# Seven quarter products in the second token-mixing product, and VectorE instructions merged over two PSUM banks or two sets

## The chip, the cores and the metric

One core of one Trainium2 chip. Times are device microseconds (us) of one execution; each quoted time is the median of the runs named beside it. PE is TensorE, DVE VectorE, ACT ScalarE, POOL GpSimd. PSUM is the memory that the kernel's matmuls write; the kernel uses it as eight banks of 512 f32 a partition. SBUF is where the kernel keeps everything else that it has on the chip.

## The reference

Eight batches of 1024 positions by 512 features. Each batch is an attention with projected keys and values, then a mixer with a token half and a channel half:

```python
k_proj = einsum('ks,bhsd->bhkd', E, k); v_proj = einsum('ks,bhsd->bhkd', F, v)
x  = softmax(q @ k_proj.T / sqrt(64)) @ v_proj          # heads side by side: (8, 1024, 512)
h  = maximum(x.T @ w_tok1, 0) @ w_tok2                  # w_tok1 1024 x 256, w_tok2 256 x 1024
u  = x + h.T
return u + maximum(u @ w_ch1, 0) @ w_ch2                # w_ch1 512 x 1536, w_ch2 1536 x 512
```

The product that this change is about is the second one of the token half, `... @ w_tok2`.

## The kernel before

A program of three layers matters here. First, every piece of work is a *job* with an engine, a price in us and a priority; a planner written in Python simulates the engines with these prices and fixes, before anything is built, one order of instructions for each engine.

```python
MM = {512: 0.216, 256: 0.109, 130: 0.057, 128: 0.057, 64: 0.057}
def pe(n, cols, fn, **kw):
    t = n * MM[cols]
    return pl.add("PE", t, t, fn, **kw)
def dve(cols, fn, ps=True, **kw):
    t = cols / 960 + 0.07 if ps else cols / 1920 + 0.07
    return pl.add("DVE", t, t + 0.09, fn, **kw)
```

Second, the two channel products and, from batch 2 on, the first token product are already done in seven quarter products where a plain blocked product has eight. This costs sums and differences of quarters: those of a weight are made once and kept in SBUF, those of the activations are made for each batch on VectorE (those for the first channel product are called S below). Several products of a set are added up in one bank; ScalarE first copies one bank into another to start it, which is called the seed copy. The sums of the first token weight, made once in batch 1:

```python
def tok1_sums():
    a11, a12, a21, a22 = [tok1_quarter(t, half) for t in range(2) for half in range(2)]
    ...
    one(5, wS[:, 0], a21, a22, add=True, after=kp_all)
    one(7, wS[:, 2], a11, a21)
    one(6, wS[:, 1], wS[:, 0], a11, deps=(5,))
    one(3, a21, a12, wS[:, 1], deps=(6, 7, 5), after=["wt1"])   # the fourth goes over a quarter of the weight
```

Third, the second token product, which is still the plain one. Output row `si` of a position takes every eighth column of the weight, so the weights have a step of 8 elements:

```python
def token2(b, si, due):
    def mm():
        for t in range(TC):                                    # TC = 2
            nc.tensor.matmul(bank(bk), wt2_sb[:, t, si::NSI], hT_sb[:, t, :], ...)   # 512 columns, NSI = 8
    pe(TC, 512, mm, ...)
    dve(512, lambda: nc.vector.tensor_add(out=u_t[b % 2][:, si, :], in0=bank(bk), in1=x_sb[:, si, :]), ...)
    # [cut] after four rows: transposition of u by DMA
```

Two other places are touched. The attention of a head is normalised in two halves (a reciprocal of 4 and a product of 256 for each), and the four sums of hidden quarters, `G`, that a set of the channel product ends with are made for one set at a time:

```python
    total(3, g21, G[:, 2, cs], True, [q21, g(2)])      # g21 has a buffer of its own
    total(5, G[:, 0, cs], g21, False, [q21, g(0)])
    total(4, G[:, 3, cs], G[:, 0, cs], False, [g(3), g(0)])
    total(6, G[:, 1, cs], G[:, 4, cs], False, [g(1), g(4)])
```

The softmax here doesn't subtract the row's maximum and nothing guards it: scores larger than these inputs give would overflow.

Of the kernel before, what the change touches and what calls it, by code (L numbers as in the profile page):

```python
# [12 lines left out]
ACT = mybir.ActivationFunctionType  # L13
EARLY = 12.0
SUMS = 60.0
FMAX = 3.4028234663852886e38

# [11 lines left out]
class Bank:  # L29


    def __init__(self, stream, full=True, seeded=False):
        self.stream, self.full, self.seeded = stream, full, seeded
        self.jobs, self.at = [], None
        self.read, self.write = [], []


class Planner:
# [37 lines left out]
    def plan(self):  # L76
# [36 lines left out]
        def home(b, now):  # L113

            if held[b.stream] == self.caps[b.stream]:
                return None
            if b.stream in "UD" and turn[b.stream][0] is not b:
                return None
            best = None
            keep = [i for i in self.homes["U"] if clean[i] and bank_free[i] is not None]  # L120
            if all(clean[:5]):
                keep = []
            for i in self.homes[b.stream]:
                t = bank_free[i]
                if t is None or (b.seeded and not clean[i]):
                    continue
                if not b.seeded and clean[i] and keep and keep[-1] == keep[0] == i:
                    continue
                c = (max(now, t), clean[i], t, i)
                if best is None or c < best:  # L130
                    best = c
            return best

        while any(can.values()):
# [26 lines left out]
            if j.takes:  # L161
                b = j.takes[0]
                b.at = spot
                turn[b.stream].remove(b)
                held[b.stream] += 1
                bank_free[spot] = None
            for b in j.banks:
                left[id(b)] -= 1
                if not left[id(b)]:
                    held[b.stream] -= 1  # L170
                    bank_free[b.at] = max(x.end for x in b.jobs) + 0.1
                    clean[b.at] = b.full
            order.append(j)
# [10 lines left out]
def kernel(  # L184
# [13 lines left out]
    nc = tc.nc  # L198
# [40 lines left out]
    def tile_of(shape, dtype, name):  # L239
        return sb.tile(shape, dtype, tag=name, name=name)  # L240

    banks = [ps.tile([P, S2], F32, tag=f"ps{i}", name=f"ps{i}") for i in range(8)]

    def bank(b):

        return banks[b.at]

# [33 lines left out]
    G_t = [tile_of([P, 7, C2, 2 * P], BF16, f"G{i}") for i in range(2)]  # L281
    a_t = [tile_of([P, S2], BF16, f"a{i}") for i in range(4)]
    rdn_t = [tile_of([P, 4], F32, f"rdn{i}") for i in range(4)]
    ub_t = [tile_of([P, 2, 2 * P], F32, f"ub{i}") for i in range(2)]
    ua_t = [tile_of([P, 2, 2 * P], F32, f"ua{i}") for i in range(2)]
    g21_t = [tile_of([P, 2, 2 * P], BF16, f"g21{i}") for i in range(2)]
    da = tile_of([P, 2, DH], F32, "da")
    ident32 = da[:KP, 0, :KP]
    db = tile_of([P, 2, DH], F32, "db")

# [285 lines left out]
    def scores(h, due):  # L576
        bk = Bank(stream[0], full=False)
        pe(
            1, 512,
            lambda: nc.tensor.matmul(  # L580
                bank(bk), kT[:, h].rearrange("p c k -> p (c k)"),
                qT[:, h].rearrange("p j s -> p (j s)"), start=True, stop=True,
            ),
            reads=[("kT", 0, h), ("kT", 1, h), ("qT", h)], takes=[bk], prio=due,
            after=[("a", h % 4)],
        )
        act(
            512,
            lambda: nc.scalar.activation(out=a_t[h % 4], in_=bank(bk), func=ACT.Exp, scale=scale),  # L589
            writes=[("a", h % 4)], uses=[bk],  # L590
        )

    def attend(h, half, due):
        bk = Bank(stream[0], full=False)
        rdn = rdn_t[2 * (h % 2) + half]

# [3 lines left out]
        def mm():  # L600
            for jj in range(2):
                j = 2 * half + jj
                nc.tensor.matmul(  # L603
                    view()[:, 2 * jj : 2 * jj + 2].rearrange("p c d -> p (c d)"),
                    a_t[h % 4][:, j * P : (j + 1) * P],
                    vb[:, h].rearrange("k c d -> k (c d)"), start=True, stop=True,
                )
# [19 lines left out]
        )  # L627

    def token1(t, due):
        bk = Bank(stream[0], full=False)  # L630
# [17 lines left out]

    def token2(b, si, due):
        bk = Bank(stream[0], full=False)  # L650

# [18 lines left out]
        if si % NJ == NJ - 1:  # L670
            i = si // NJ
            j = sp(
                3.5,
                lambda: nc.sync.dma_start_transpose(
                    out=uT_t[i].rearrange("p s dc q -> p (s dc) q"),
                    in_=u_t[b % 2][:, i * NJ : (i + 1) * NJ].rearrange("p s d -> p (s d)"),
                ),
                reads=[("u", b % 2, n) for n in range(i * NJ, (i + 1) * NJ)],
                writes=[("uT", i, n) for n in range(HP)], prio=None,
            )  # L680

            if b > 1:
                j.lat += 3.0
            turned_u[b, i] = j

# [49 lines left out]
    def token1_seven(b, due):  # L735
# [35 lines left out]
        def product(n):  # L771
            bb = bk["y" if X_OF[n] == "y" else "x"]
            src = rows[n] if n in T else xs[{1: 11, 2: 21, 3: 22}[n]]
            w = [("wS", n)] if n in (5, 6, 7, 3) else ["wt1"]
            pe(
# [40 lines left out]
        product(4)  # L816
        both(1, 0, ub, rows[6][0])

    def token1_pair(hp, due):
# [103 lines left out]
    def up_set(j, m):  # L923
# [3 lines left out]
        bk = {n: Bank("U", seeded=n == "y") for n in "xyz"}  # L927
        ub, ua, g21 = ub_t[s % 2], ua_t[s % 2], g21_t[s % 2]

# [41 lines left out]

        def total(n, in0, in1, add, deps):
            f = nc.vector.tensor_add if add else nc.vector.tensor_sub
            dve(
                512, lambda: f(out=G[:, n, cs], in0=in0, in1=in1), ps=False, reads=deps,  # L975
                writes=[g(n)],
            )
# [18 lines left out]
        relu(1, "y")  # L996
        product(4)
        dve(
            512, lambda: add_relu(g21, view("z"), ub), reads=[("ub", s % 2)],
            writes=[("g21", s % 2)], uses=[bk["z"]],  # L1000
        )
        q21 = ("g21", s % 2)
        total(3, g21, G[:, 2, cs], True, [q21, g(2)])
        total(5, G[:, 0, cs], g21, False, [q21, g(0)])
        total(4, G[:, 3, cs], G[:, 0, cs], False, [g(3), g(0)])
        total(6, G[:, 1, cs], G[:, 4, cs], False, [g(1), g(4)])

    out_v = out.rearrange("b (p si) d -> b p si d", p=P)

    def down_block(j):  # L1010
# [63 lines left out]
        def add_u(dst, key, src, sh, dh):  # L1074
# [3 lines left out]
            )  # L1078

        product(1, 0)  # L1080
        act(
# [5 lines left out]
        if last:  # L1087
            return finish(p6, product, add_u, store, bk, view, o_of, o_key)
        add_u(db, "db", "y", 1, 0)
        product(2, 3)  # L1090
        add_u(o_of(0, 0), o_key(0, 0), "x", 0, 0)
        product(5, 4)
        dve(
            512, lambda: nc.vector.tensor_add(out=da, in0=view("y"), in1=u_of(1, 1)),
            reads=u_key(1), writes=["da"], uses=[bk["y"]],
        )
        dve(
            512, lambda: nc.vector.tensor_add(out=o_of(1, 1), in0=view("z"), in1=da),
            reads=["da"], writes=[o_key(1, 1)], uses=[bk["z"]],
        )  # L1100
        product(3, 5)
        add_u(o_of(0, 1), o_key(0, 1), "y", 0, 1)
        store(0)
        product(4, 6)
        dve(
            512, lambda: nc.vector.tensor_add(out=o_of(1, 0), in0=view("z"), in1=db),
            reads=["db"], writes=[o_key(1, 0)], uses=[bk["z"]],
        )
        store(1)

    def finish(p6, product, add_u, store, bk, view, o_of, o_key):
# [12 lines left out]
        follow(p5[0], p6[1])  # L1124
        add_u(da, "da", "y", 1, 1)
        da_w = add(da, "da", "w", da, "da")
        follow(product(2, 4)[0], p5[1])
        c22 = add(o_of(1, 1), o_key(1, 1), "z", da, "da")
        store(1, (1,))
        follow(add_u(dc, ("ub", 0), "y", 0, 1), da_w)  # L1130
        follow(add_u(db, "db", "y", 1, 0), c22)
        follow(add_u(o_of(0, 0), o_key(0, 0), "x", 0, 0), c22)
# [4 lines left out]
        product(4, 6)  # L1137
        add(o_of(1, 0), o_key(1, 0), "z", db, "db")
        store(1, (0,))
# [36 lines left out]
    def front(b, begin, end):  # L1176
# [20 lines left out]
        for h in range(H):  # L1197
            if h + 2 < H:
                unit(0.4, lambda t, h=h: scores(h + 2, t))
            for half in range(2):  # L1200
                unit(0.25, lambda t, h=h, half=half: attend(h, half, t))
# [3 lines left out]
        else:  # L1205
            unit(3.2, lambda t: token1_seven(b, t))
        for si in range(NSI):
            unit(0.55, lambda t, si=si: token2(b, si, t))
        total = sum(c for c, _ in units)
# [8 lines left out]
    for b in range(B):  # L1218
# [5 lines left out]
        if b == 1:  # L1224
            tok1_sums()
        if b + 1 < B:
            at = 2 * TU * (b + 1)
# [58 lines left out]
```

## Time and profile before

| | before |
|---|---|
| time | 423.75 us (423.72 to 423.80, 3 runs) |
| TensorE | 413.8 us busy, 98% of the span |
| VectorE | 341.3 us busy, 81%, 837 instructions |
| ScalarE | 227.1 us busy, 54% |
| waits of TensorE from 110 us on | none listed |

The lines are in the prediction below. Read them so: the row of tenths says where in the span an engine is full, the chain of waits says which engine the end depends on, and a table of stretches gives busy time of each engine in a part of the span. Records of TensorE overlap (four matmuls of 256 columns are recorded as 0.60 us, and the next begins 0.44 us after their start), so I go by starts: what a start comes later than 0.109 us (after a matmul of 256 columns) or 0.215 us (after one of 512) is a wait. I call this the excess of a matmul.

### The profile page before, as it was taken

What the parts mean: (1) busy time and instruction counts of PE and PEld (TensorE: products, weight loads), DVE (VectorE), ACT (ScalarE), POOL (GpSimd) and SP (SyncE); (2) the same over time, 40 slices, a digit from 0 to 9 for tenths busy, and PEclk for the clock granted to TensorE, in tenths of its full rate; (3) what the DMA queues carried; (4) which work ended last, traced back from release to release, by engine and by line L of the source; (5) the groups of instructions that cost most, each with busy time, mean ns of one, the idle gap of its engine ahead of it and who ended that gap; (6) DMA issues with size and microseconds to landing.
All of it is one profiled execution on the core that took longest, in us unless ns stands there. A gap on an engine that the chain in (4) does not pass through costs nothing.

```text
span 421.8 us, 9380 instructions
## 1 busy us (share of the span) xinstructions
PE 413.8 (98%) x3778; PEld 343.0 (81%) x3778; DVE 341.3 (81%) x837; ACT 227.1 (54%) x434; POOL 66.3 (16%) x104
## 2 busy tenths in 40 slices
PE   8899999999999999999999999999999999999996
PEld 4587887788788878888788877889788888888885
DVE  2469979689799978799779887899778897878684
ACT  2858885357656454655446455564636544354430
POOL 8453220021111211020121200220100100010010
PEclk9999999999999999999999999999999999999999
DMA  9999999979999889959987699979930502250223
GB/s 168 207 201 206 207 207 165 240 121 209 173 155 219 138 192 176 151 152 149 202 139 158 110 169 225 146 156 152 200 75 2 151 2 99 51 151 6 95 96 106
DMA packets 96651, 62.47 MB, mean 148 GB/s; under 512 B 62048, under 2 KB 92256, under 8 KB 96608
## 3 DMA queue, kind: packets, MB, share of 16 engines
q0 software_dynamic: 34944, 45.09, 54.2%
q1 hardware_dynamic: 61584, 16.52, 22.5%
q8 instruction: 29, 0.48, 0.5%
q10 hardware_dynamic: 80, 0.26, 0.2%
q14 instruction: 14, 0.11, 0.1%
HBM read 59.24 MB, written 16.78 MB: 180 GB/s over the span
## 4 chain that ended last, share of the span: by engine, by line
PE 88%; DVE 5%; DMA 4%; POOL 1%; issue 1%; ACT 0%; POOLq 0%; DVEq 0%
PE ps L1041 34%; PE ps L940 33%; PE ps L654 6%; PE ps L764 4%; PE ps L603 3%; PE ps L580 3%; DMA q_sb<-in_q_dram 3%; PE ps L467 3%; DMA v_sb<-in_v_dram 2%; DVE u L867 1%; PE ps L634 1%; DVE x_sb L620 1%; PE ps L564 1%; DVE u L746 1%; PE ps L470 0%
## 5 line engine op out<-in xcount | busy, mean ns | idle before, releaser
L1041 PEld LDWEIGHTS <-G 128*128 128x128 bf16 x1344 | 129.8, 98 | 18.8 <-issue 0.3
L1041 PE MATMUL ps<-wc_sb,G 128*128 128x256 bf16 x768 | 103.1, 273 | 0.1
L962 ACT ACTIVATE G<-ps 128x512 bf16<-128x512 f32 x96 | 57.0, 597 | 70.6 <-PE ps L940 70.3
L940 PEld LDWEIGHTS <-wc_sb 128*128 128x128 bf16 x768 | 74.3, 98 | 12.0 <-issue 0.2
L1041 PE MATMUL ps<-wT,G 128*128 128x256 bf16 x576 | 77.7, 273 | 0.0
L940 PEld LDWEIGHTS <-wT 128*128 128x128 bf16 x576 | 55.3, 98 | 10.3 <-issue 1.0
L940 PE MATMUL ps<-uT,wc_sb 128*128 128x256 bf16 x384 | 57.7, 273 | 0.0
L940 PE MATMUL ps<-S,wc_sb 128*128 128x256 bf16 x384 | 57.6, 273 | 0.0
L940 PE MATMUL ps<-S,wT 128*128 128x256 bf16 x384 | 54.7, 273 | 0.4 <-DVE S L697 0.4
L1070 POOL DMA_DIRECT2D out_dram<-o x30 | 16.3, 545 | 219.8 <-DVE o L1076 133.5
L620 DVE TENSOR_TENSOR x_sb<-ps,rdn 128x256 bf16<-128x256 f32 x128 | 49.9, 416 | 0.6
L968 ACT COPY ua<-ps 128x512 f32<-128x512 f32 x48 | 28.2, 587 | 32.6 <-PE ps L940 32.2
L589 ACT ACTIVATE a<-ps 128x512 bf16<-128x512 f32 x64 | 37.3, 599 | 14.6 <-PE ps L580 14.1
L665 DVE TENSOR_TENSOR u<-ps,x_sb 128x512 bf16<-128x512 f32 x56 | 36.3, 686 | 10.2 <-PE ps L654 9.8
L921 DVE CUSTOM_DVE_ANT_0 g<-ps,ub 128x512 bf16<-128x512 f32 x48 | 32.9, 687 | 11.8 <-PE ps L940 11.6
L921 DVE CUSTOM_DVE_ANT_0 G<-ps,ua 128x512 bf16<-128x512 f32 x48 | 32.8, 684 | 10.4 <-ACT ua L968 10.4
L975 DVE TENSOR_TENSOR G<-G 128x512 bf16<-128x512 bf16 x96 | 39.4, 420 | 1.8
L615 DVE RECIPROCAL rdn<-ps 128x4 f32<-128x4 f32 x128 | 20.7, 175 | 15.5 <-PE ps L603 13.3
L968 ACT COPY ub<-ps 128x512 f32<-128x512 f32 x48 | 28.1, 586 | 9.0 <-PE ps L940 8.6
L603 PE MATMUL ps<-vb,a 128*128 128x130 bf16 x256 | 31.2, 220 | 0.0
L981 ACT COPY ps<-ps 128x512 f32<-128x512 f32 x48 | 27.8, 580 | 5.5 <-PE ps L940 3.1
L654 PE MATMUL ps<-hT_sb,wt_sb 128*128 128x512 bf16 x112 | 29.9, 379 | 0.0
(90 smaller groups left out, 527.3 us busy)
## 6 DMA issues: line engine op xcount, KB each, us to landing
out_dram<-o POOLq DMA_DIRECT2D x30, 512.0 KB, 4.0
k_sb<-in_k_dram POOLq DMA_DIRECT2D x14, 512.0 KB, 7.7
v_sb<-in_v_dram POOLq DMA_DIRECT2D x14, 512.0 KB, 9.7
q_sb<-in_q_dram POOLq DMA_DIRECT2D x14, 512.0 KB, 9.7
wc_sb<-in_moe_w_ch_dram POOLq DMA_DIRECT2D x6, 256.0 KB, 12.3
wc_sb<-in_moe_w_ch_dram POOLq DMA_DIRECT2D x4, 384.0 KB, 12.2
k_sb<-in_k_dram POOLq DMA_DIRECT2D x4, 256.0 KB, 6.7
v_sb<-in_v_dram POOLq DMA_DIRECT2D x4, 256.0 KB, 7.2
```

The source lines that it names most:

```text
L589: lambda: nc.scalar.activation(out=a_t[h % 4], in_=bank(bk), func=ACT.Exp, scale=scale),
L603: nc.tensor.matmul(view()[:, 2 * jj : 2 * jj + 2].rearrange("p c d -> p (c d)"), a_t[h % 4][:, j * P : (j + 1) * P], vb[:, h].rearrange("k ...
L620: lambda: nc.vector.tensor_tensor(out=x_sb[:, 4 * half : 4 * half + 4, h * D : (h + 1) * D], in0=view()[:, :, 0:D], in1=rdn[:, :, None].to ...
L654: nc.tensor.matmul(bank(bk), wt2_sb[:, t, si::NSI], hT_sb[:, t, :], start=(t == 0), stop=(t == TC - 1),)
L665: lambda: nc.vector.tensor_add(out=u_t[b % 2][:, si, :], in0=bank(bk), in1=x_sb[:, si, :]),
L921: nc.vector._custom_dve(TENSOR_ADD_SAT, out=out, in0=in0, in1=in1, s0=FMAX, s1=0.0)
L940: nc.tensor.matmul(t[:, c, :], w1_of(n, dd, 2 * m + c), a_of(j, n, dd), start=(n in (1, 7) and c == 0 and dd == 0), stop=(c == 1 and dd == 1),
L962: lambda: nc.scalar.activation(out=G[:, n, cs], in_=view(src), func=ACT.Relu),
L968: 512, lambda: nc.scalar.copy(out=dst, in_=view("y")), writes=[(name, s % 2)],
L975: 512, lambda: f(out=G[:, n, cs], in0=in0, in1=in1), ps=False, reads=deps,
L981: 512, lambda: nc.scalar.copy(out=view("y"), in_=view("x")), takes=[bk["y"]],
L1041: nc.tensor.matmul(view(where[n])[:, t, :], G[:, G_OF[n], cc, t * P : (t + 1) * P], w2_of(n, cc), start=(n in opens and t == 0 and cc == 0 ...
```

## The change

Its intent: TensorE sets the time, so take columns away from it. The second token product of batches 3 to 7 goes to seven quarter products of half the columns, in two sets of rows. That gives VectorE more to do, and to make room its other instructions are merged: a head's attention is normalised over two PSUM banks in one go, two rows of the plain second product are added in one go (batch 2), and the sums of `G` are made for two sets at once. For the two-bank instructions all of PSUM becomes one tile; for room in SBUF four buffers go (`da`, `db` and two of `g21`), and `g21` is computed in place in `G[5]`.

```diff
-        q21 = ("g21", s % 2)
-        total(3, g21, G[:, 2, cs], True, [q21, g(2)])
...
+        both = TOTALS[m] if SINGLE <= j < NSB - 1 else (m,)
+        if both:
+            total(3, 5, 2, True)
+            total(5, 0, 5, False)
...
+    wt2_v = wt2_sb.rearrange("p t (a i sh r) -> p t i sh r a", i=2, sh=2, r=2)
+    def tok2_sums():
+        for i in range(2):
+            a11, a12, a21, a22 = [wt2_v[:, t, i, sh] for sh in range(2) for t in range(2)]
+            def one(n, out, in0, in1, add=False, deps=(), after=(), i=i):
+                dve(512, lambda: f(out=out, in0=in0, in1=in1), ps=False, prio=SUMS + 50, ...)
+            waits = [("wait", 0), ("wait", 1)]
+            one(5, wS2[:, 0, i], a21, a22, add=True, after=waits)
+            one(7, wS2[:, 2, i], a11, a21, after=waits)
+            one(6, wS2[:, 1, i], wS2[:, 0, i], a11, deps=(5,), after=waits)
+            one(3, a21, a12, wS2[:, 1, i], deps=(6, 7, 5), after=["wt2"])
...
+    def token2_set(b, i, due, ...):
+        product(1); act(512, copy of x's bank into y's bank)
+        product(7); product(6); from_x(kept[0], ..., "y", 1, 0)
+        product(2); ...; product(5); ...; product(3); ...; product(4); ...
...
+            if b >= WHOLE:                      # WHOLE = 3
+                unit(0.5, lambda t, h=h: attend_whole(h, t))
...
+        if b == 2:
+            tok2_sums()
```

(The lines of `token2_set` are shortened here.) Three of the four sums of a set go into `wS2`, which shares its bytes with the buffer `wait`; the fourth goes over a quarter of the weight itself. `wait` is in use by the output blocks of the first batches, so the sums can only come when these are through with it.

## The prediction

> **What bounds the kernel now**
>
> I read the page first (busy shares, slices, chain), then the table of stretches, then the list of waits, then two short pieces of the timeline for the real cost of one instruction. From the page:
>
> ```profile
> PE 413.8 (98%) x3778; PEld 343.0 (81%) x3778; DVE 341.3 (81%) x837; ACT 227.1 (54%) x434; POOL 66.3 (16%) x104
> PE   8899999999999999999999999999999999999996
> DVE  2469979689799978799779887899778897878684
> ...
> PE 88%; DVE 5%; DMA 4%; POOL 1%; issue 1%; ACT 0%; POOLq 0%; DVEq 0%
> PE ps L1041 34%; PE ps L940 33%; PE ps L654 6%; PE ps L764 4%; PE ps L603 3%; PE ps L580 3%; DMA q_sb<-in_q_dram 3%; PE ps L467 3%; DMA v_sb<-in_v_dram 2%; DVE u L867 1%; PE ps L634 1%; DVE x_sb L620 1%; PE ps L564 1%; DVE u L746 1%; PE ps L470 0%
> ```
>
> TensorE (PE) is busy from the second slice to the last but one, and 88% of the chain that ended last is its matmuls. VectorE (DVE), which most of the diff is about, has 5% of that chain. The DMA share of the chain is the first 24 us (loads of k, v, q), which the change leaves alone.
>
> Busy is not dense, since PE records overlap. So the table of stretches, one of 49 us for each batch, which is the period of the kernel:
>
> ```profile
> 110.00:159.00 49.00, 49.00 (x434) 40.06 (x432) 42.31 (x105) 26.96 (x51) 6.70 (x10) 1.00 0.95 177
> 257.00:306.00 49.00, 49.00 (x444) 41.50 (x443) 41.77 (x102) 26.74 (x50) 6.72 (x10) 1.00 0.91 171
> 306.00:355.00 49.00, 49.00 (x439) 42.15 (x437) 42.19 (x104) 25.00 (x47) 2.13 (x4) 1.00 0.24 69
> ```
>
> The columns are window, length, then PE, PEld, DVE, ACT, POOL busy, then clock, DMA share and GB/s. PE has no gap in 49 us, at full clock; DVE has about 42 of 49 (86%). DMA share falls from 0.91 to 0.24 in the last stretch and the PE does not go faster for it, so the loads don't pace it either. The list of waits, asked for PE alone from 110 us to the end, names no wait at all.
>
> The timeline of PE shows how dense it is:
>
> ```profile
> 304.13 0.60 PE L764 MATMUL ps<-u,wt_sb 128*128 128x256 bf16 x4
> 304.57 1.04 PE L940 MATMUL ps<-S,wT 128*128 128x256 bf16 x8
> 305.44 0.82 PE L1041 MATMUL ps<-wc_sb,G 128*128 128x256 bf16 x6
> 306.10 1.46 PE L654 MATMUL ps<-hT_sb,wt_sb 128*128 128x512 bf16 x6
> 307.39 0.27 PE L940 MATMUL ps<-S,wc_sb 128*128 128x256 bf16 x1
> ```
>
> Take starts, not durations: eight 256-column matmuls in 305.44 - 304.57 = 0.87 us, 0.109 us each; six of 512 columns in 307.39 - 306.10 = 1.29 us, 0.215 us each. That is what the PE pays for a column whatever the product. The same reading for DVE:
>
> ```profile
> 328.48 0.42 DVE L975 TENSOR_TENSOR G<-g,G 128x512 bf16<-128x512 bf16 x1
> 328.81 0.69 DVE L1106 TENSOR_TENSOR o<-ps,db 128x512 f32<-128x512 f32 x1
> 329.41 0.17 DVE L615 RECIPROCAL rdn<-ps 128x4 f32<-128x4 f32 x1
> 329.50 0.40 DVE L975 TENSOR_TENSOR G<-G 128x512 bf16<-128x512 bf16 x1
> 329.81 0.18 DVE L615 RECIPROCAL rdn<-ps 128x4 f32<-128x4 f32 x1
> 329.90 0.73 DVE L620 TENSOR_TENSOR x_sb<-ps,rdn 128x256 bf16<-128x256 f32 x2
> 330.54 0.42 DVE L975 TENSOR_TENSOR G<-G 128x512 bf16<-128x512 bf16 x1
> ```
>
> Start to start: 512 bf16 within SBUF 0.33 us, 512 from PSUM 0.60, a reciprocal of 4 about 0.09, 256 from PSUM 0.32. About 0.09 us of each recorded duration lies under the next instruction. So merging two DVE instructions saves less than the durations suggest.
>
> [...] Splitting one of 512 in two costs only some 2 ns, so a product with 7/8 of the columns costs nearly 7/8 of the time.
>
> [...] The second token product takes its weights with a step of 8 elements, and its weight loads last longer (the L654 PEld group has 144 ns, the others 98 ns). Under a 215 ns matmul that hides; under 109 ns it might not. The trace has the harder case: L855 uses the same strided weights with 128-column matmuls, and the chain of waits has it at 16 in 0.98 us, 0.061 us each. So at 109 ns it is hidden.
>
> ```profile
> 26.42 0.98 PE ps L855 x16
> ```
>
> [...]
>
> **The change part by part**
>
> PE. The second token product (L654) of batches 3 to 7 goes to seven quarter products in two sets. Before, per batch: 8 x 2 = 16 matmuls of 512, 16 x 0.215 = 3.44 us. After: 2 sets x 7 products x 2 = 28 of 256, 28 x 0.109 = 3.05 us. Saved 0.39 us, times five batches 1.95 us. Nothing else on the PE changes: the merged attention keeps its four matmuls a head, and the instruction lists have 3838 matmuls against 3778, exactly 5 x (28 - 16) more. The first token product was already in seven parts from batch 2 on. All of the 1.95 us lies on the path.
>
> DVE occupancy, start to start; [...]256 bf16 at 0.20, 1024 bf16 at 0.60 (as the first token product's differences have it):
> - Attention over two banks, 40 heads: before 2 x (0.09 + 0.32) = 0.82, after 0.09 + 0.60 = 0.69. Saves 0.13 x 40 = 5.2 us.
> - Sums of G over two sets, 13 blocks: before 12 x 0.33 = 3.96, after 4 x 0.60 + 4 x 0.33 = 3.72. Saves 0.24 x 13 = 3.1 us.
> [...]
> - Seven products, 5 batches: before 8 x 0.60 = 4.80; after 4 differences x 0.20 + 12 additions from PSUM x 0.60 = 8.00. Adds 3.2 x 5 = 16 us.
> - Sums of the second weight, once, 8 strided instructions of 256 elements[...]: 8 x 0.33 adds 2.6 us.
>
> Sum: +10 us of DVE over the run. Per batch from 3 on: -1.0 -0.5 +3.2 = +1.7 us, so from 42 of 49 to about 44 of 48.6, or 90%. The instruction count falls (837 to 749 in the lists), but the load rises: the merging pays for half of what the seven products cost. ACT gains one copy of 0.58 us a set, 5.8 us in all, at 54% load.
>
> Path: 423.75 - 1.95 = 421.8. I add 0.2 us for new short waits in ten sets: 422.0.
>
> **The rivals**
>
> 1. DVE becomes the bound. At 90% it isn't on average. But the second token product crowds the last fourth of a batch's preparation: 8.0 us of its own in about 12 us, beside a base (up, down and S sums, about half of DVE's time) of 6 us, so about 2 us too much there. If the PE had to wait for it in each of the five batches: 421.8 + 5 x 2 = 432, slower by 2%. Against: u is needed late. In the trace the first transposition of u is issued at 309.2 us, lands 4.2 us later, and the first S sum that reads it starts at 320.0, over 6 us of slack; and the next batch's projection, which follows, needs no DVE. Partly true would be 0.3 us a batch, 423.3.
>
> 2. The seeded chain. In each set one PSUM bank is filled, read, added to, read and added to again, so three products of a set each wait for a DVE or ACT read of 0.6 us plus signalling. Ten sets x 4 turnarounds x 0.3 us exposed would be 12 us, 434. Against: the order of the PE's instructions puts 4 to 18 other matmuls (0.4 to 2 us) between most dependent products, and the first token product has the same chain now and shows no wait.
>
> 3. The saving is hidden, because loads or something else sets the period: 423.75, no change. Against: no PE wait from 110 us on, and the transfers wait for buffers that PE frees.
>
> 4. The rearrangement also removes the small PE waits before 110 us (some 1.6 us between 40 and 113 us by starts). Then 420.5 or so. Only the plan of batch 2 changes there, so I give it little.
>
> **Range and chances**
>
> The saving is known to a tenth; what is open is the waits, more likely added than removed. Predicted 422.0 us, 421.0 to 423.6 in 8 of 10. Faster by over 2% would need 8.5 us, which the change takes nowhere: 0.5%. Slower by over 2% needs rival 1 or 2 at nearly full size: 2.5%. Within 2%: 97%.
>
> **What would show it right or wrong**
>
> Right: 3838 PE instructions, L654's 112 replaced by 32 of 512 (batches 1 and 2) and 140 of 256 at 0.109 start to start; a period of about 48.6 us from batch 3 on; PE still without waits; DVE busy up by 5 to 12 us with 749 instructions. Wrong: the new 256-column matmuls at more than 0.11 us (strided weights not hidden); PE waits for DVE u or for ACT's seed; an S sum that waits for the transposition of u; DVE without idle time in the last fourth of a batch.

VectorE's load was summed to +10 us: -5.2 for the attention, -3.1 for the sums of `G`, -0.3 for batch 2's rows in pairs (an addition of 1024 elements from PSUM), +16 for the seven products and +2.6 for the sums of the second weight. The trace after has 1.15 us from the start of such an addition to that of the next instruction (115.92 to 117.07 us), so the pairs save 4.80 - 4 x 1.15 = 0.2. Of the prices, the 2 ns for splitting a matmul are the difference of two of 256 columns (2 x 0.87 / 8 = 0.2175 us) and one of 512 (0.215); the 0.20 us of 256 bf16 was an estimate, and the trace after has 0.20 (starts at 257.15 and 257.35 us); the 0.33 us of a strided sum was an estimate with no measurement behind it.

## The result, and the profile after

| | before | after |
|---|---|---|
| time, same session | 423.77 us (423.72 to 423.84, 4 runs) | 425.26 us (424.97 to 426.20, 4 runs) |
| VectorE busy, instructions | 341.3 us, 837 | 351.1 us, 749 |
| ScalarE busy | 227.1 us | 232.3 us |
| matmuls in the instruction list | 3778 | 3838 |
| first weight load of a channel up product to last one of a down product | 385.12 us | 386.32 us |

The ratio is 1.0039, with a 95% interval of 1.0021 to 1.0056. Ratios here are the mean time of one kernel's runs over that of the other's of the same rounds, so not quite the ratio of the medians quoted. Executions over 1.5% slower than the fastest of the same kernel are left out of the means. On another chip, as a control, the changed kernel gave 425.61 us against 423.65, 1.0043 (1.0031 to 1.0056). So the change costs about 1.6 us where I had predicted that it saves 1.75.

The last row of the table is what I compare traces by. It leaves out the first 32 us, which are mostly loads and differ by some tenths from run to run (the stretch begins at 32.07 us before and at 32.35 after), and the tail. In it the change costs 1.2 us in the first pair of traces and in the control's trace. Each value is one trace; how far two traces of one kernel can lie apart is said at the repeated run below.

The changed kernel's page, the lines that answer to those of before (busy, rows of tenths, chain):

```profile
PE 412.1 (97%) x3824; PEld 347.0 (82%) x3838; DVE 351.1 (83%) x749; ACT 232.3 (55%) x444; POOL 66.2 (16%) x104
PE   9899999999999998999999999999999999999996
DVE  2369979779679899999998799797988999887684
PE 85%; DVE 7%; DMA 4%; issue 1%; ACT 1%; POOL 1%; POOLq 0%; DVEq 0%
```

TensorE's row has one new 8, in the sixteenth slice (159 to 169 us); VectorE is at 9 there, in the slice before it and in the five after it. VectorE's share of the chain that ended last grew from 5% to 7%. (14 of the 3838 matmul records are missing from this trace, which is why the page counts 3824.)

The table of stretches (window, length, then PE, PEld, DVE, ACT, POOL busy, clock, DMA share, GB/s), first one line of the kernel before, then two of the changed kernel:

```profile
159.00:208.00 49.00, 49.00 (x440) 41.26 (x438) 42.31 (x104) 27.03 (x51) 6.72 (x10) 1.00 0.92 160
```

```profile
159.00:208.00 49.00, 47.68 (x439) 41.21 (x441) 46.41 (x96) 26.39 (x50) 6.13 (x9) 1.00 0.84 158
...
306.00:355.00 49.00, 48.82 (x454) 43.22 (x454) 44.49 (x93) 27.25 (x53) 2.14 (x4) 1.00 0.33 88
```

Before, VectorE had 42.31 of 49 us in the stretch from 159 us and TensorE all 49.00. Now VectorE has 46.41 and TensorE lacks 1.3. In the later stretch VectorE has 44.49, near the 44 that the prediction worked out, and TensorE lacks 0.2. In the three stretches not shown TensorE lacks 0.5 (110 to 159 us, into which the first of the waits below reaches), 0.3 and 0.1. So most of the loss sits in and just before one stretch. The list of waits of TensorE from 110 us on, empty before, now has three lines (who waited, for what; us in total, times, longest):

```profile
PE psum L848 <- DVE hT_sb L1126: 1.1, 1, 1.1
PE psum L965 <- DVE hT_sb L1126: 0.5, 1, 0.5
PE psum L1250 <- ACT psum L1301: 0.2, 1, 0.2
```

The timeline of TensorE there (start, length, instruction, then the idle time before it and who ended it):

```profile
158.01 0.61 PE L1145 MATMUL psum<-S,wT 128*128 128x256 bf16 x4
159.74 0.60 PE L848 MATMUL psum<-x_sb,wt_sb 128*128 128x256 bf16 x4 [1.13 <-DVE hT_sb L1126]
...
162.68 0.61 PE L1145 MATMUL psum<-S,wc_sb 128*128 128x256 bf16 x4
163.81 0.38 PE L965 MATMUL psum<-hT_sb,wt_sb 128*128 128x256 bf16 x2 [0.52 <-DVE hT_sb L1126]
```

By starts: four matmuls from 158.01 should end in 0.44 us and took 1.73, an excess of 1.29; four from 162.68 took 1.13, an excess of 0.69. Together 2.0 us. And VectorE just before:

```profile
155.09 1.15 DVE L916 TENSOR_TENSOR wait<-wt_sb 128x256 bf16<-128x256 bf16 x2
156.14 0.64 DVE L916 TENSOR_TENSOR wait<-wait,wt_sb 128x256 bf16<-128x256 bf16 x1
156.67 0.63 DVE L916 TENSOR_TENSOR wait<-wt_sb 128x256 bf16<-128x256 bf16 x1
157.20 1.34 DVE L916 TENSOR_TENSOR wt_sb<-wt_sb,wait 128x256 bf16<-128x256 bf16 x1
...
159.26 0.43 DVE L1126 CUSTOM_DVE_ANT_0 hT_sb<-psum,u 128x256 bf16<-128x256 f32 x1
```

L916 is the sums of the second weight. They begin at 155.09 and, with one instruction between them, hold VectorE until 160.48. The instruction that TensorE waits for at 159.26 (a part of the hidden token layer, needed by the first token product's next job and by the new second product) stands behind seven of the eight. A sum that reads the strided weight starts its successor after 0.52 to 0.64 us, one that also writes it in place after 0.90. Start to start the eight take 5.06 us, where the prediction had 8 x 0.33 = 2.6.

### The profile page after: what moved, and what is told of

Same layout as the page of the kernel before. It is cut to its first block, busy times and chain, and to the rows that moved or that the text cites. A ratio compares the mean times of both kernels' runs of the same rounds, so it can differ in the third digit from the quotient of the medians.

```text
span 423.2 us, 9409 instructions
## 1 busy us (share of the span) xinstructions
PE 412.1 (97%) x3824; PEld 347.0 (82%) x3838; DVE 351.1 (83%) x749; ACT 232.3 (55%) x444; POOL 66.2 (16%) x104
## 4 chain that ended last, share of the span: by engine, by line
PE 85%; DVE 7%; DMA 4%; issue 1%; ACT 1%; POOL 1%; POOLq 0%; DVEq 0%
PE psum L1250 33%; PE psum L1145 32%; PE psum L965 4%; PE psum L848 3%; DMA q_sb<-in_q_dram 3%; PE psum L597 3%; PE psum L484 3%; PE psum L656 2%; DMA v_sb<-in_v_dram 1%; DVE G L1181 1%; PE psum L620 1%; DVE u L1072 1%; DVE G L1126 1%; PE psum L687 1%; PE psum L711 1%
## 5 line engine op out<-in xcount | busy, mean ns | idle before, releaser
L1250 PE MATMUL psum<-wc_sb,G 128*128 128x256 bf16 x768 | 102.5, 273 | 0.3 <-ACT psum L1301 0.2
L1167 ACT ACTIVATE G<-psum 128x512 bf16<-128x512 f32 x96 | 57.2, 599 | 58.7 <-PE psum L1145 58.2
L1250 PE MATMUL psum<-wT,G 128*128 128x256 bf16 x576 | 77.2, 273 | 0.4 <-ACT psum L1301 0.2
L1181 DVE TENSOR_TENSOR G<-G 128x512 bf16<-128x512 bf16 (+1 forms) x140 | 69.7, 518 | 0.9
L1145 PE MATMUL psum<-uT,wc_sb 128*128 128x256 bf16 x384 | 57.8, 273 | 0.1
L1145 PE MATMUL psum<-S,wc_sb 128*128 128x256 bf16 x384 | 57.6, 273 | 0.2
L1145 PE MATMUL psum<-S,wT 128*128 128x256 bf16 x384 | 54.6, 273 | 0.4 <-DVE S L781 0.4
L1126 DVE CUSTOM_DVE_ANT_0 G<-psum,ub 128x512 bf16<-128x512 f32 x48 | 32.9, 686 | 12.3 <-PE psum L1145 12.1
L606 ACT ACTIVATE a<-psum 128x512 bf16<-128x512 f32 x64 | 36.5, 601 | 9.2 <-PE psum L597 7.9
L1285 DVE TENSOR_TENSOR o<-psum,u 128x512 f32<-128x512 f32 x55 | 37.7, 686 | 4.5 <-PE psum L1250 4.5
```

The costliest lines, as they stand in the source:

```text
L606: lambda: nc.scalar.activation(out=a_t[h // 2 % 2][:, h % 2], in_=bank(bk), func=ACT.Exp, scale=scale),
L1126: nc.vector._custom_dve(TENSOR_ADD_SAT, out=out, in0=in0, in1=in1, s0=FMAX, s1=0.0)
L1145: nc.tensor.matmul(t[:, c, :], w1_of(n, dd, 2 * m + c), a_of(j, n, dd), start=(n in (1, 7) and c == 0 and dd == 0), stop=(c == 1 and dd == 1),
L1167: lambda: nc.scalar.activation(out=G[:, n, cs], in_=view(src), func=ACT.Relu),
L1181: 512 * len(both), lambda: f(out=G[:, n, c], in0=G[:, a, c], in1=G[:, b, c]), ps=False,
L1250: nc.tensor.matmul(view(where[n])[:, t, :], G[:, G_OF[n], cc, t * P : (t + 1) * P], w2_of(n, cc), start=(n in opens and t == 0 and cc == 0 ...
```

## The experiments

All were run against the kernel before on the same chip, in up to five rounds (4 to 6 runs of the kernel tried, 11 of the kernel before); before's median was between 423.52 and 423.79 us on the chips used. "The stretch" is the last row of the table above, 385.12 us before and 386.32 after.

### Theory A against theory B

**Theory A**: the sums of the second weight, twice as long as priced and put into the fullest part of the run, make TensorE wait 2 us; the rest of the change does roughly what was predicted. **Theory B**: VectorE's greater load as a whole, or the new products' chain of banks, costs the time, and the sums only mark the place.

*The sums made tiny.* The order of all instructions is kept, each sum works on 8 elements where it had 256, and the products take other weights. Its output is wrong, which doesn't matter for the time.

```diff
-    512, lambda: f(out=out, in0=in0, in1=in1), ...
+    512, lambda: f(out=out[:, :, :4], in0=in0[:, :, :4], in1=in1[:, :, :4]), ...
-    return wS2[:, {5: 0, 6: 1, 7: 2}[n], i, r]
+    return wS[:, {5: 0, 6: 1, 7: 2}[n], 2 * i + r]
```

> The changed kernel with the eight sums of the second token weight cut to 8 elements each, the matmuls taking other finite weights in their place (wrong result on purpose; the order of all instructions is the same). Theory A, the one-off sums at the fullest place of VectorE (4.9 us of it between 155 and 160.5 us, PE then idle 1.1 and 0.5 us and 2.0 us over by start-to-start): 423.3 us, 2.0 below the changed kernel's 425.3, with no PE wait over 0.5 us between 155 and 165 us. Theory B, the loss is spread over batches 3 to 7 by VectorE's higher load and the seeded chain: 425.0 or more, sums or no sums.

Measured 423.35 us, ratio 0.9995 (0.9983 to 1.0007), the stretch 384.39. The two waits are gone and about 2 us with them.

*The sums on dense operands.* Same order and same number of elements, only the strided quarters are read (and the fourth written) as if they lay together. Its output is wrong, which doesn't matter for the time.

```diff
-            a11, a12, a21, a22 = [wt2_v[:, t, i, sh] for sh in range(2) for t in range(2)]
+            a11, a12, a21, a22 = [
+                wt2_sb[:, t, (2 * i + sh) * 2 * P : (2 * i + sh + 1) * 2 * P].rearrange("p (r a) -> p r a", r=2)
+                for sh in range(2) for t in range(2)
+            ]
```

> The changed kernel with the same eight sums of 256 elements, but on operands without the step of 8 (wrong result on purpose; same order of instructions). If the stride is what made the sums dear: each 0.20 to 0.28 us instead of 0.53 to 0.90, together about 2 us, and 423.4 to 423.8 us. If eight instructions with their own waits are dear whatever the stride: each 0.5 us or more, and 424.8 to 425.3.

Measured 422.94 us, ratio 0.9985 (0.9973 to 0.9997), the stretch 384.44. The view of the sums' line gives their durations (least, median, greatest):

```profile
L919 DVE TENSOR_TENSOR wait<-wt_sb x4: 286/292/295, 155.2 to 156.2; 128x256 bf16<-128x256 bf16 x4
...
L919 DVE TENSOR_TENSOR wt_sb<-wt_sb,wait x2: 293/293/293, 156.0 to 157.0; 128x256 bf16<-128x256 bf16 x2
```

The same view of the changed kernel has these two kinds at 626 and 1322 ns in the median. So an instruction of 256 elements lasts 0.29 us dense, 0.63 with a step of 8 in what it reads and 1.32 when it writes with that step too, and the step alone is worth the 2 us. By starts the dense sums follow each other in 0.20 us, 1.6 us for the eight.

*Only the merging*, without seven products and without sums. With the seven products gone, rows of the second product are added in pairs in all batches from 2 on (24 such instructions, where the changed kernel has 4):

```diff
-        if b < 3:
+        if b < B:
...
-        if b == 2:
-            tok2_sums()
```

> The changed kernel without the seven products of the second token product and their sums; attention over two banks, pairs of rows in the second token product from batch 2 on and doubled sums of G stay. VectorE about 333 us busy instead of 351, PE 3778 matmuls. Theory A and B both: no PE work saved, 423.5 to 423.8, as the kernel before. Rival C, the merged instructions themselves make PE wait (two banks held at once, sums of G later): 424.5 or more.

Correct; 423.80 us, ratio 1.0002 (0.9990 to 1.0014). VectorE's busy time fell by 13.0 us (341.3 to 328.3) and the time did not move: taking load off VectorE gained nothing here.

*Only the seven products*, without merging (`WHOLE = TWO = SINGLE = 99`):

> The changed kernel with all merging switched off; seven products in the second token product of batches 3 to 7 and their sums stay. VectorE about 359 us busy. Theory A: the same one-off loss and the same saving, 425.0 to 425.5. Theory B: VectorE is about 2 us a batch fuller still, 426.5 to 429. Rival C: 424.2 or less, as the merging was the harm.

Correct; 426.79 us, ratio 1.0077 (1.0065 to 1.0089). Two waits at the sums are there again, 0.94 and 0.91 us in the timeline, and some 0.7 us more within 10 us after. Merging was worth 1.5 us, but this does not say yet that it is worth it away from the sums.

### Moving the sums

Theory A says a correct kernel can have the 2 us back if the sums lie where VectorE is idle. The first tries let the planner do it: `wait` is left to the sums from the start (`EARLY_O = 0`), the fourth sum gets room of its own, the price goes to the measured 0.55 us, and the priority to about 90 us.

```diff
-EARLY_O = 4
+EARLY_O = 0
...
-                    512, lambda: f(...), ps=False, prio=SUMS + 50,
+                    922, lambda: f(...), ps=False, prio=80 + 3.5 * next(turn),
...
-            one(3, a21, a12, wS2[:, 1, i], deps=(6, 7, 5), after=["wt2"])
+            one(3, wS2[:, 3, i], a12, wS2[:, 1, i], deps=(6,))
```

> The changed kernel, correct, with the eight sums of the second token weight made earlier (from about 90 us on, when VectorE has room) into memory that is free by then, the fourth also into its own dense place, and told to the planner at 0.55 us each. Theory A: the waits of 2 us at 158 to 164 us go and none comes instead: 423.2 to 423.6 with the kernel before at 423.5 to 423.8, so 1.7 to 2.0 below the changed kernel. If the 4.9 us of VectorE only move their harm: 424.5 to 425.3.

Correct, and worse: 428.21 us (4 runs), ratio 1.0108 (1.0090 to 1.0126). A miss, and an instructive one. The three longest lines of the list of waits of TensorE from 110 us on:

```profile
PE psum L964 <- DVE a L994: 1.7, 4, 0.6
PE psum L656 <- DVE x_sb L673: 0.9, 3, 0.3
PE psum L1249 <- DVE o L1284: 0.8, 1, 0.8
```

The waits for `hT_sb` are gone as theory A says, but other prices made the planner choose another order for the whole run, with other waits. That is a confound of my own making, so from here on I either kept the changed kernel's order or took parts out of this one.

*The same with the sums on GpSimd* (priced 1.0 us each):

> The same, but with the eight sums on GpSimd, which is 16% busy. Theory A: the same 423.2 to 423.6, VectorE about 5 us less busy. If GpSimd's work slows VectorE's instructions beside it or holds up the loads that GpSimd issues: 424 or more, with VectorE's 512-element instructions longer than 0.42 us in that stretch.

Correct, 432.47 us (429.83 to 436.17), ratio 1.0208 (1.0161 to 1.0256), another miss. Its runs fall into two groups, 429.8 to 430.3 and 434.6 to 436.2, and the profile is of the shortest. That profile shows nearly the same waits as the one before, so what the longer runs lost stays open; the next run on GpSimd shows a cost of that place.

*The early sums on VectorE with a buffer of its own for `g21` in the last block* (and another order of the four sums of `G` there), to take away a wait of 0.28 us at 414 us:

```diff
-    512, lambda: add_relu(G[:, 5, cs], view("z"), ub), reads=[("ub", s % 2)],
+    512, lambda: add_relu(G[:, 5, cs] if j < NSB - 1 else g21, view("z"), ub), reads=[("ub", s % 2)],
```

> The early sums, and in the last block the old separate buffer for the one sum that the change now overwrites in place (the order of its four sums then lets the one come first that the last product's second part waits for). The start-to-start gap of 0.28 us at about 410 us, which the changed kernel and all runs so far have and the kernel before has not, goes: 0.2 to 0.4 us below the early sums alone, 422.9 to 423.3.

Correct, 428.37 us, ratio 1.0106 (1.0090 to 1.0122): no difference from the kernel without the buffer.

*Early sums, no merging* (`WHOLE = TWO = SINGLE = 99` on top of the early sums):

> Seven products without any merging, but with the early sums. If the merging matters only because it makes room around the one-off sums: 423.2 to 423.8, as the early sums with merging. If VectorE's load in batches 3 to 7 costs by itself (theory B as a second part): 424.3 to 425.5, with PE waits on VectorE in several batches.

Correct, 423.89 us, ratio 1.0001 (0.9987 to 1.0014), and only one wait of 0.6 us is listed for TensorE from 110 us on; the stretch is 384.67. VectorE is busy for 358.8 us here, 7.7 more than in the changed kernel, and the ratio is lower (1.0001 against 1.0039 and 1.0043; with the sums at their late place the same kernel without merging had 1.0077). This falsifies the load half of theory B, and shows that the bad order of the run with early sums comes with the merging.

*The changed kernel's exact order with the sums on GpSimd* (with `after_again` as a control):

```diff
-                f = nc.vector.tensor_add if add else nc.vector.tensor_sub
+                f = nc.gpsimd.tensor_add if add else nc.gpsimd.tensor_sub
```

> The changed kernel itself once more, beside the next two on one chip: 1.0039 times the kernel before as at first, so 424.9 to 425.5.

> The changed kernel, correct, with nothing changed but the engine of the eight sums: GpSimd, which has nothing to do between 155.4 and 179.8 us in the changed kernel's trace; the order of all other instructions stays the same, which the early sums did not keep. At the 0.8 us each that GpSimd took for them before: done by about 162 us, before the first set's second product needs them. Theory A: no PE wait at 158 to 164 us, 1.5 to 2.0 us below the changed kernel, 422.9 to 423.6. If the early sums' 428 came from the moved sums as such and not from the other order that they brought: 425 or more.

Correct, 428.68 us (426.54 to 428.80), ratio 1.0106 (1.0090 to 1.0122): 3 us worse than the changed kernel, a miss. The timelines of VectorE, GpSimd and TensorE show one place:

```profile
157.76 4.81 DVE L943 TENSOR_TENSOR u<-hT_sb 128x256 bf16<-128x256 bf16 x1 [1.22 <-ACT hT_sb L874]
```

```profile
156.41 1.77 POOL L916 TENSOR_TENSOR wait<-wt_sb 128x256 bf16<-128x256 bf16 x2
...
162.49 1.61 POOL L916 TENSOR_TENSOR wt_sb<-wt_sb,wait 128x256 bf16<-128x256 bf16 x1
```

```profile
164.86 1.03 PE L1145 MATMUL psum<-S,wc_sb 128*128 128x256 bf16 x4 [2.43 <-DVE S L781]
```

The VectorE instruction of 157.76 lasts 0.28 us elsewhere (the view of its line has a median of 284 ns); here it lasts 4.81, until GpSimd is nearly through with its sums, and TensorE waits 2.43 us for what follows it. It runs beside GpSimd's sums (156.41 to 164.10 us); what slows it down is not shown. The sums themselves are no faster on GpSimd: 655 to 1160 ns each where they read with the step, 1343 to 1607 ns where they also write with it. (The run that has them early on GpSimd shows 785 ns for the fourth sum written densely.) After the wait the next 12 matmuls of 256 columns take 2.79 us by starts (164.86 to 167.65 us), 0.23 us each and not 0.109, so that some 1.5 us more are lost there; why, is not shown.

*The same with the tail's buffer*:

> As the run before, and in the last block the separate buffer of the kernel before for the sum now overwritten in place: order of instructions unchanged. 0.2 to 0.4 us less, 422.6 to 423.3, without the gap of 0.28 us in the last block.

Correct, 427.94 us (426.56 to 429.49), ratio 1.0100 (1.0084 to 1.0116). It cannot be told from the run before.

*Which merging makes the early order bad?* Early sums, once with the attention in halves and the double sums of `G`, once with the two-bank attention and single sums of `G`:

```diff
-WHOLE = 3
+WHOLE = 99
```

> The early sums on VectorE (428.2 us), but attention one bank at a time as in the kernel before; doubled sums of G stay. If the two-bank attention is what made that order bad (PE waited 0.45 us for its VectorE read in three batches, and its set chain 0.54 us): 423.5 to 425. If the doubled sums of G, or the plan as a whole: 426 or more.

```diff
-SINGLE = 2
+SINGLE = 99
```

> The early sums (428.2 us) with G's sums one set at a time as in the kernel before; two-bank attention stays. Without both mergings it was 423.9, without the attention's 427.4. If the doubled sums of G are what makes that order bad (VectorE busy without a gap at 366 to 383 us, PE waiting): 423.5 to 424.8. If neither alone does: 426 or more.

Both correct. With attention in halves 427.38 us, ratio 1.0085 (1.0072 to 1.0098); with single sums 423.26 us, ratio 0.9997 (0.9984 to 1.0009), the stretch 384.49. So the early order is bad with the doubled sums of `G` and not without them. Each switch also lets the planner choose a new order, so whether the instructions or the order chosen with them do the harm is not separated. An argument, not shown: a doubled sum can only start when the later set is done, and it holds VectorE for 0.60 us at a time where a single one holds it for 0.33.

*The test that keeps the changed kernel's order.* After planning, only the four sums of the first set are moved, into an idle gap of VectorE of 2.46 us that ends at 114 us; they get 2 KB a partition of their own. The second set's sums stay where they were, and no fourth sum is written over the weight any more. (The 2.3 us of the expectation for the dense sums is the sum of their durations; by starts it is 1.6.)

```diff
+    own = tile_of([P, 4, 2, P], BF16, "own")
...
-            one(3, a21, a12, wS2[:, 1, i], deps=(6, 7, 5), after=["wt2"])
+            one(3, wS2[i][:, 3], a12, wS2[i][:, 1], deps=(6, 7, 5), after=["wt2"])
...
-    plan = pl.plan()
+    plan = [j for j in pl.plan() if j not in early]
+    at = [n for n, j in enumerate(plan) if j.eng == "DVE"][222]
+    plan[at:at] = early
```

> Correct. The changed kernel in its own order but for four of the eight sums: the first set's are put, on VectorE, into its idle gap that ends at 114.7 us in the changed kernel's trace, into 2 KB of own memory; the second set's stay at their place; the fourth sum of each goes to a dense place. Left at 155 to 160 us: 4 x 0.53 = 2.1 us of sums, about what the dense sums had there (2.3 us). Theory A: as the dense sums, 0.998 to 0.9995 times the kernel before, 422.7 to 423.4, and no PE wait over 0.5 us at 155 to 165 us. If it is not the sums' VectorE time at that place: 424.5 or more.

Correct; 423.30 us, ratio 0.9991 (0.9979 to 1.0003), the stretch 384.39. The timelines of VectorE and TensorE of this kernel, where the long wait was:

```profile
156.99 0.41 DVE L1130 CUSTOM_DVE_ANT_0 hT_sb<-psum,u 128x256 bf16<-128x256 f32 x1
157.32 0.60 DVE L918 TENSOR_TENSOR wait<-wt_sb,wait 128x256 bf16<-128x256 bf16 x1
```

```profile
158.29 0.61 PE L1149 MATMUL psum<-S,wT 128*128 128x256 bf16 x4
158.74 0.60 PE L850 MATMUL psum<-x_sb,wt_sb 128*128 128x256 bf16 x4
```

`hT_sb` now comes at 156.99 in place of 159.26, and TensorE goes on after 0.45 us in place of 1.73. A correct kernel has the 2 us back by these two edits, four sums moved and the fourth sums written densely (ratio 0.9991 in place of 1.0039 and 1.0043, the stretch 1.93 us shorter). With the two runs above that are wrong this confirms theory A. Repeated on another chip beside the last experiment:

> The kernel e13 once more, as the anchor of the run before it on the same chip: 423.1 to 423.6 by every theory, ratio 0.998 to 1.0005.

423.52 us (6 runs), ratio 0.9998 (0.9986 to 1.0010). Its profiled run was one of the long ones (424.06), with a wait of 0.73 us for the transposition of the projected keys at 84 us, and its stretch is 385.38. So two traces of one program can differ by 1.0 us in the stretch: its differences of 2 us are borne out by the medians, those of some tenths are no more than a reading of single traces.

### The rest of the loss

With the sums repaired the kernel is only level with before; 0.74 us of the predicted 1.95 is left in the stretch (385.12 to 384.39; the traces of the kernels with tiny sums, with the tail's buffer and with the swaps have 384.3 to 384.5). What ate the other 1.2? The trace lists new excesses of TensorE: 0.38 us at 210 us (a seed copy of a down product on ScalarE, behind a cast), 0.32 at 257 and 0.32 at 305 (a new product asks for a PSUM bank that a projection still holds: in the changed kernel's trace it starts at 258.00 us, just after ScalarE's casts of a projection end at 257.95), 0.28 at 410 (in the last block, where `g21` in place makes the first two sums wait for each other: the second starts 0.46 us after the first, and 0.34 us in the kernel before) and 0.27 near 185.

*The tail's buffer with the repaired sums*:

> The run before with the separate buffer in the last block as well: 0.2 to 0.4 us less, 422.4 to 423.1, the fastest correct version so far; the gap of 0.28 us in the last block gone.

Correct, 423.34 us, ratio 0.9999 (0.9985 to 1.0014). The excess at 410 fell from 0.28 to 0.16 us in the trace, and the time did not move by anything that these runs resolve. The expectation is missed.

*The tail's buffer with early sums and no merging*:

> Seven products with early sums and no merging (423.9 us), with the separate buffer in the last block: 0.2 to 0.4 us less, 423.3 to 423.8.

Correct, 425.35 us (423.50 to 426.68), ratio 1.0028 (1.0008 to 1.0048). The runs fell into two groups and the profile into the longer one, with a wait of 2.0 us at 111 us for the load of a later batch's v. Inconclusive.

*Neighbours swapped in the repaired kernel's order*, so that the bank and the seed copy come in time:

```diff
+    for p in sevens:                       # a set's seventh product, one TensorE job later
+        n = plan.index(p)
+        m = next(m for m in range(n + 1, len(plan)) if plan[m].eng == "PE")
+        if p not in plan[m].deps and not set(p.banks) & set(plan[m].banks):
+            plan.insert(m, plan.pop(n))
+    for a in seeds:                        # the seed copy, ahead of a cast
+        ...
```

> The kernel e13 (half of the sums early) with two kinds of neighbours swapped in its order: set 0's seventh product comes one block of TensorE's work later in every batch, so that it no longer asks for the PSUM bank that a projection still holds, and in batch 4 the seed copy of the down product goes ahead of a cast on ScalarE. Theory A (what is left of the loss is these small new waits of TensorE: 0.38 us near 210, 0.24 and 0.08 near 257 and again near 306): 0.6 to 1.0 us below e13, 422.3 to 422.9, and no wait of TensorE over 0.2 us near those times. Rival (the waits only move to the next product, since TensorE is that far ahead of ScalarE there anyway): 423.1 to 423.6, with waits of the same sum within 3 us after the old places.

Correct, 423.21 us, ratio 0.9985 (0.9972 to 0.9997), against 423.52 for the anchor on the same chip; the stretch 384.48, no shorter than the 384.39 of the anchor's first trace. The timeline of TensorE, first of the kernel with the sums repaired, then with the swap as well:

```profile
255.90 0.38 PE L969 MATMUL psum<-hT_sb,wt_sb 128*128 128x256 bf16 x2
256.36 0.38 PE L969 MATMUL psum<-u,own 128*128 128x256 bf16 x2
256.57 0.60 PE L1149 MATMUL psum<-S,wT 128*128 128x256 bf16 x4
```

```profile
255.99 0.60 PE L1152 MATMUL psum<-S,wT 128*128 128x256 bf16 x4
256.43 0.38 PE L969 MATMUL psum<-u,own 128*128 128x256 bf16 x2
256.85 0.38 PE L969 MATMUL psum<-hT_sb,wt_sb 128*128 128x256 bf16 x2
```

Two matmuls should take 0.22 us. In the first they take 0.46 ahead of the seventh product (`u,own`); in the second the seventh product comes in time, but 0.42 passes ahead of the next one. The wait moved on, from 0.24 to 0.21 us. At 210 us the excess of 0.38 became 0.08 and 0.18 within 2 us, with one of 0.07 at 218.6. Over the three places the excess fell by 0.1 us in all, and 423.21 against 423.52 is not resolved, as the intervals of the ratios overlap. So the rival of that run holds: these waits are not the accident of one pair of neighbours.

## Why the prediction was right or wrong

**Right: the saving on TensorE.** 140 matmuls of 256 columns start 0.109 us apart in the median, and the strided weights (144 ns a load against 98) are hidden, as the prediction read from L855.

**Right: rival 1 and rival 2 at their full size did not come.** VectorE's list of waits from 110 us on names no transposition of u, a kernel with 7.7 us more of VectorE's work was not slower (the early sums without merging), and in the repaired kernel the turnarounds of a set cost some tenths, not 12 us.

**Right in the total, in part by luck: VectorE's load.** +10 us predicted, +9.8 measured. The run without merging gives the parts: the seven products and the sums add 18.8 us of busy time (341.3 to 360.1; predicted 16 + 2.6 = 18.6), and merging takes 9.0 off (360.1 to 351.1; predicted 8.6). (The 13.0 of the run with merging alone are no test of the 8.6, as that run pairs rows in six batches and not in one.) But the prediction added up start-to-start times and busy time adds up recorded durations, and the sums in it take 5.06 us and not 2.6. That the totals agree said nothing of this term.

**Wrong, the step that failed: the sums of the second weight, "8 x 0.33 adds 2.6 us."** The term was mis-sized: 5.06 us start to start. The 0.33 was my estimate for a strided operand, near the 0.32 that before's trace has for 256 elements from PSUM, and I measured nothing; the sums of the first token weight, the nearest thing in the trace of before (512 elements, 426 ns each), read their quarters without such a step. What had to be measured is the step: a sum of 256 elements starts its successor after 0.20 us on dense operands, after 0.53 where it reads with a step of 8 and after 0.90 where it also writes with it (the dense run and the changed kernel). By what the step costs this, no run shows. And I entered the term only in a sum over the run; the path ("423.75 - 1.95 = 421.8") has no wait for it. It is paid once, in one go, and it lies between 155 and 160.5 us, directly ahead of an instruction that TensorE needs. In that stretch VectorE went to 46.4 of 49 us, not to the 44 of the average. The kernel's own planner has the same price for them, 512 / 1920 + 0.07 = 0.34 us each. That the price put them there is not shown: they also need the buffer `wait`, whose last reader starts at 153.89 us, 1.2 us before the first sum. Cost: two excesses of TensorE of 1.29 and 0.69 us, 1.9 us in the stretch (386.32 to 384.39), 2.0 to 2.3 us in the medians (425.26 and 425.61 to 423.30, on different chips).

**Wrong in size: "I add 0.2 us for new short waits in ten sets."** With the sums repaired, 1.95 - 0.74 = 1.2 us of the saving is still missing in the stretch. The excesses listed above add up to 1.6 us, less 0.3 of small ones that before had near 205 and 254 us and that are gone: about 1.3. Short new waits were the prediction's mechanism; their sum is six times the 0.2. Only two of the five, 0.32 each, lie in the ten sets where it put them. The others are at a seed copy of a down product (0.38), in the last block through `g21` in place (0.28) and near 185 us (0.27). That they make up the loss is read from the trace and not shown by a run that takes them away: the swaps only moved them, and the tail's buffer nearly halved one without a measurable gain.

**Rival 1's partial form** ("0.3 us a batch, 423.3") is near the repaired kernel's time, but that is luck: the largest waits of the repaired kernel come from ScalarE and from PSUM banks, not from VectorE's load: without the merging, at 7.7 us more VectorE work, the stretch is hardly longer (384.67 against 384.39).

**What stays open.** Why the doubled sums of `G` do no such harm in the changed kernel's order, while the order with early sums is 5 us longer with them (428.21 against 423.26); and whether any order exists in which the 1.2 us come back. The best correct kernels, the one with half of the sums early (423.30 and 423.52), the same with swaps (423.21) and the one with single sums of `G` (423.26), are between 0.9985 and 0.9998 of before: they repair the change, and do not beat the kernel before by anything worth having.

## What to carry to other kernels

A cost that is paid once still has a place: look at which engine is full in the few microseconds where it lands and what stands behind it in that engine's queue, not at its share of the run. Price an operand by how its elements lie in memory, as a trace shows it (256 elements here: 0.20 us dense, 0.53 read with a step of 8, 0.90 written with it too), or lay out the weight once so that its quarters are dense (the dense run shows what that would be worth; no correct kernel tried it); a planner believes its prices. And when TensorE has no slack, 0.4 us saved a batch is no more than one or two new waits of 0.2 to 0.4 us, so count the new hand-overs between engines with the measured size of such a wait before counting columns.
